# The last 64 tokens of a batch on both partition halves, from q@kv to x, and weights loaded by chunk halves

## The chip, the cores and the metric

The kernel runs on one core of a Trainium2 chip. The metric is the device time of one execution in microseconds (us). Before the change the median of 13 runs is 226.29 us, from 224.67 to 227.38.

## What is computed

Shapes: q, k, v are (8 batches, 8 heads, 576 tokens, 64). Linear attention without a softmax is normalized per head and token, the heads are joined to x (8, 576, 512), and x goes through an attention of four experts, of which each token takes the best two.

```python
kv = np.einsum('bhsd,bhse->bhde', k, v)
out = np.einsum('bhsd,bhde->bhse', q, kv)
rms = np.sqrt(np.mean(out * out, axis=-1, keepdims=True) + 1e-06)
x = (out / rms * g_norm).transpose(0, 2, 1, 3).reshape(B, S, H * D)

logits = x @ w_gate                      # (B, S, 4), the best two kept, softmax over them
for e in range(4):
    qe, ke, ve = x @ wq[e], x @ wk[e], x @ wv[e]          # 512 -> 64
    a = causal_softmax(qe @ ke.transpose(0, 2, 1) / 8)
    result += weight_of_expert_e * (a @ ve @ wo[e])
```

## The kernel before

The work is written as small tasks, each named by its kind, batch and part: `("out", b, i)` is q@kv of token block `i` of batch `b`. Three strings, found by a planner ahead of time, fix everything that a scheduler would decide: `ORDER` is the sequence in which all tasks are emitted (the order on each engine's queue follows from it), `ENGINE` gives one letter per task (V VectorE, A ScalarE, G GpSimd) for those that can run on more than one, and `SLOTS` the PSUM bank or buffer that each takes. `ZEROS` puts matmuls of zeros ahead of some tasks on TensorE. Tasks of several batches are interleaved.

The 576 tokens of a batch are four blocks of 128 and a last one of 64 (block index `NF` = 4, length `REM` = 64). The stages of a batch, with the names used by the profile:

- Loads: `lk`, `lv`, `lq` and the remainders `lkr`, `lvr` are DMAs issued by SyncE (SP), for batch 0 those of v by ScalarE. The weights are loaded once, during the first batches: `lw(nm, p)` loads the experts 2p and 2p+1 of wq, wk or wv into `w_stage`, and `ws` scales them by `g_norm` into `w_r`.
- `kv` (L405) sums k^T v over the tokens; `kvc`, `kgm`, `kgr`, `kgx` copy it into `kvx` with four gate columns per head (64 + 4 = 68 = `GW`). `kvx` holds each pair of heads (c, c+4) on the two partition halves with zeros in the other head's columns, so one matmul against 136 columns serves both heads.
- `q` (L448) and `qc` bring q to `qT`, with heads c and c+4 on the partition halves of chunk c. For batches from 2 on, `qc` alone does this by a VectorE transpose (L456).
- `out` (L466): per block four matmuls, one per chunk c, into two PSUM banks. The last block has 64 tokens, so its chunks 0, 1 go to partitions 0 to 63 and its chunks 2, 3 to 64 to 127. An fp32 matmul is two PE instructions in the profile.
- `oc` copies the block to `o_sb` (tokens on partitions; L283 is the ScalarE form of every such copy, L285 the VectorE form). For the last block these are two copies of 64x272, both into partitions 0 to 63. `sq` (L492, L496 on ScalarE, L498 on GpSimd) squares, `red` (L502) sums to `ms`.
- `ln`, `rs`, `na` to `nd` make 1/rms (`rstd`) of all blocks. `gl` and `lg` (L545, L551) make the gate's logits in `lg8`: gate columns times `rstd`, summed over the eight heads. Then `m8` (L584) finds the best two, and `sh`, `ex`, `md`, `mk`, `gt`, `den`, `rd`, `gate` make the weights that `iv` (L727) needs, after the scores of the batch.
- `xm` (L557, GpSimd) multiplies by `rstd` and permutes the features so that chunk c of x holds the features 4p + c; `x` (L567) transposes each chunk on TensorE by a matmul against the identity, and `xc` copies to `xT`.
- `v` (L626), `qp` and `kp` (L645) project x; `sc` (L672) are the scores, `exp` (L686) on ScalarE, `msk` (L692) on GpSimd, `pv` (L706), `rc`, `iv`, `oc2` (L723, L727, L734) scale, `ot` (L749) transposes, `y` (L764) projects out, `yc` copies, `st` stores.

For a block of 64 tokens `x` moves 64 columns in each of its four matmuls:

```python
p_t[:, c * P : c * P + nt], lhsT=tiles["x", b, i][:, c, :], rhs=ident_r[:, 0:nt], start=True, stop=True
```

and `proj` reads `xT` chunk by chunk against `w_r[nm][:, c, ...]`, so the order of features in x and in the weights' rows must agree.

Of the kernel before, what the change touches and what calls it, by code (L numbers as in the profile page):

```python
# [24 lines left out]
ZEROS = {("q", 0, 4): 8, ("gb",): 2, ("kv", 0, 2): 6, ("kv", 0, 1): 3, ("q", 0, 3): 3}  # L25

ORDER = (
    "090E010403080507020u060H0v003F0D0c0A0F0G3C0b0J0I0d0C0a0j0i0B0e0f0k390s0g3H0l0m0h0t381A0n163B1C1B1D0w3718170o19"
    "0y3A0x1Q0q1R0p0z1S1T3Y0U1U0r0+1V3Z3E1k1E1F1G12100-1H5f1h1I111l143U1m3G1J131Y151i3V3D1K1j1Z1L1M3L1a0S1N1O3K5g0V"
    "3I1P1W3S5l1b1X0K1n3J3T0Q1e3W3M3N0M3Q5i1q1o1r1p3X0T1c5e3O1f1s201g3P225c213q1d0L1+233r3R5d3e0R1-1t3a0N3f1u5b3g3i"  # L30
    "1v3b3h3m3c0W3s3d2W3j5j3t3n243k2X0O3o3l2UAS3p253u1y2V1w5h1z3v3w2e1x3x5r3y2f5m3z2b460X2Y2h885s2c4C5p2i2Z5k0P5q40"
    "4D5t5uAV474E4926485v8C43418D274A5w423+4S4B2d5n3-2E2g4T2H284F2F442a864I4U4G2I4J4H5y2G452B5o292k4V4K2j4L5x4Q2J2C"
    "2A2l802m4M2n4N4a2o4R2D2p2q2r2L0Y4b2KAR2P4Y2M2Q2N2R2O4y4Z854l4z4c4m814i4d4n4f5z4+5+4j844e5-4g4k4-89630Z4h836059"
    "6450615A535156826B6562575B6766525487586C6F68552SAa6D6G2s4O2T2t4W6H8A6E692x4X6A344P2yAZ316I4p35324o2z6J4t8H6K4u"
    "4q4v6L364r8G6M4s6N8N8F6O6d338E8MAX4w8I6X2+4x8B8J6e2-5D6U6f6Y308K2u6R6ZAW6V5H2v6t8L5I6a6W5J6S2w6u5CAT6T6P6r5E5F"
    "6Q6b6s6p6g6cCt6x5G6j6h6q6k6v6i6y8P6l7N6w6m8O7P7OCz6n8UAc6o7QAe8Y8VAU8W7a8Z7X7b7R7Y8Q7c8XAd7S7Z7U8R8g8a7TAY5K7V"
    "8b6-8hAb8S7W8c5L8i708TC-7d8d8j7e8e6z7fCs7i7j8f7gAi6+7hCxAh8k7k8l7A8m77Ao8n7BC+748o7C7871An8pAgCy8yAq72AfAp92Cv"
    "5Y758zAk8-7l5Z93Aj8+5V5a948v5PAl905QFU8q9I915W5R8s8wAm9J9K5X8x7m73Av8r769LCw7995AzAw9896D199977DAx9A8t9BCuA+7F"
    "Ay7GAr8uA-7H9C9QAs9DD0B0AtB59RFM7EAuB17ID3B67J9q7KHjB7DD9OB8B2HkD59rB3D69PD7HiB49bDC9YB99c9VBA9Z9d9SD2D4BB9T9a"
    "9ED8FHBC9oD99WBD9UBE9G9FBFFQDABT9M7L5M7M9HFJBN5S9p5NBU5T9N7wBQBGBV9-5UDB9s7xA09vBK9tBW9y7yDE7q9wBXBOBZDF5OBHBL"  # L40
    "BPBRHlBMBaA1DK9XBS9u9zBj9xDLHm9eBk9+9f7r9gDOFLBYDM9jA2BbDP7sA39k9hFODNBlDQBIFRA7A4BmBc9lDSA8DRA5BJFIBdA9BpBeDT"
    "A69iBnBqFKBhBoCFBiHnDGCGDWFTDHCDDXHqDIDJDYBfHuCEDUDZAA9mBg7nAB9nCQFPDVCNCRCK7oCSCOCHFXFNCICPFW7pFYCLCJFVFSDaCM"
    "ALDbFZDcCTDdFaAMHoCUDeACDfCYDlAFFbANAD7tAGBrDgAECVFcCWDhCZDiCaAHHyCXBsHxHr7uDoHzFeDuC07vDxBwC1FgBzBxHvBtDyFdD+"
    "HwDrB+FfDvHtD-AIH+ByBuFlB-DwAJHpDzC2FtE0H-BvAKC3FuE1FmC4HsFpI0FnFhFqE2FoE3FrFxI1C8C5C9FiC6FsAOFy7zFjAPDsCA7+AQ"
    "C7CbFzDpDtFkCBCc7-DmI3FvDqEAF+CCDjFwE8DkCgF-E9CpG0DnChCmI2CqCiG1EgCnG2I4CrG3G4I5CdG5EhCoEGEBG7CeG6CfGMCjGAEHI6"
    "CkGPGNIAClGQI7GOGJEEIBI8IMEFICECINI9ERGREDGDELIDESEOGSEMEIGTE6IOEJGKGUIEIPGGGLEPEeEKENIFEQE7IIEfIGETE4IHIJErE5"
    "ElIKEsEiEmEoEVEtILEjEUEnEZGEEaEWEbIQEXGBEpEkEYGHEcGFEqG8GIGCGZEdIRG9GbISGaITGXIUGcIVGdGYIWGVIbIXGfGeInIYGWH3Gg"
    "IqIoIrIpIkEvH4EuEzH5IsEwE+ItExE-IeEyIlH6IuF0IvIcImIhF1HGIdH7HHHAH8HIHDFEHEF5H9FFIyFGF6HBHFF8IzFBF9F7HCF2FCIiFA"
    "IZFDIjIfIaGhIgF3IwGiJ0F4IxGsJ1GpGtGjGqGuGmJWGkGrJ6GnJXGlJYGoJ7I+JZJ2I-J4J3GwJ5GvG+HKG-GxH0GyJHGzJaJIHJHOJbJJJj"
    "HPHLJgHQHMJkHNJcJhJBJlJEHRJCJiH1J8HSH2JFJDJdHfJ9JGHWHgHcHhJeJAHZHdJLHaJfHeJKHXJPJmJQHbJMJRJnJNJoHYJOJpJUHTJqJS"  # L50
    "JVJrJuJTJsHUJvJtHVJ-K2K0JwJyJxK1K3K8K4JzK5J+K6K7K9KA"
)
ENGINE = (
    "VAVAVAVAVAVVVVVVVVVVVGVVVVVGVGVVVAVAVVVVAVVVVVVVVAVAVAVAVAVVAVVVAVVAAVVVAVVAAVAAAGAGAAGGAGAAGGAGGVGVVGVVGVVGVV"
    "GVVVGAGGGVVGVVVVVVVVVVVVVVVAGVAGVAGVAGVVVGVVGVVVVAVVVAGVAGVAGVAGVVVGVVGVVAVAVVAVVAVVAVVVVVVVVVVVVVVVVVVVAVVAVV"
    "VAVAVVVVVAAVVAAVVAAVVAAVVAAVAAGGGGGVGVAGVAGVAGVAGVAVGAGGGVVGVAVAVVVVVAVAVVVAGVAGVAGVAGVVVGVVGVVAVVVVVAGVAGVAGV"
    "AGVVVGVVGVVVVAVVAVVAVVVVVAVVVVVVVVVVVVVVVVVVVAVVAVVVVVAGVVVGVVAAVVVGVVAGVAAGGGGGVGVAGVAGVAGVAGVAVGAGGGVVGVVVVV"
    "AVVVAVAVAVAGVAGVAGVAGVVVGVVGVVAVVVVVAGVAGVAGVAGVVVGVVGVVVVVVVAVVAVVVVVAVVVVVVVVVVVVVVVVVVVVVVVVVVVVVAVVAGVVVAV"
    "VAGVVVGVAAGGAGGVGVAGVAGVVGVAGVAVGAGGGVVGVVVVVVVVVVVVVVVAGVAGVAGVAGVVVGVVGVVAVVVVVAGVAGVAGVAGVVVGVVGVVVVAVVAVVV"
    "VVAVVVVVVVVVVVVVVVVVVVVVVAVVAVVVVVVGVVAAVVAGVVVAVVVAVAAAGGGGVGVAGVAGVAGVAGVAVGAGGGVVGVAVAVAVAVAVVVVVAGVAGVAGVA"  # L60
    "GVVVGVVGVVAVAVVVAGVAGVAGVAGVVVGVVGVVAVAVVAVVAVVAVVAVVVVVVVVVVVVVVVVVVVVVVAVVVVVAAVVVGVVVGVVAGVVVAVAAAGAGGVGVVG"
    "VVGVAGVAGVVVGAGGGVVGVVVAVAVVVAVVVVVAGVAGVAGVAGVVVGVVGVVVVVVAVAGVAGVAGVAGVVVGVVGVVVVVVVVVVVVVVVVVVVVVVVVVVVVVVV"
    "VVVVVVVVAVVVVVAGVVVGVVAAVVAGVVAGVAAAGAGGVGVVGVAGVAGVVGVAVGAGGGVVGVVVAVAVVVVVAVAVAGVAGVAGVAGVVVGVVGVVVVVVAVAGVA"
    "GVAGVAGVVVGVVGVVVVAVVAVVAVVVVVVVVVVVVVVVVVVVVVVVVVVVVVVVVVVVGVVAGVVAAVVAGVVAGVAAGGGGGVGVVGVVGVVGVVGVVVGAGGGVVG"
    "VAVVVVVAVVVAVAVAGVAGVAGVAGVVVGVVGVVVVVVVVAVAGVAGVAGVAGVVVGVVGVVVVAVAVVAVVVVVAVVVV"
)
# [9 lines left out]
def names(nb):  # L76
# [3 lines left out]
    for b in range(nb):  # L80
# [14 lines left out]
        out += [(m, b, g) for g in range(len(PARTS[b])) for m in ("ln", "rs", "na", "nb", "nc", "nd")] + [("gl", b), ("lg", b)]  # L95
# [23 lines left out]
def kernel(  # L119
# [61 lines left out]
    g_rows = const.tile([P, NCH], FP32, name="g_rows")  # L181
# [29 lines left out]

    kr, vr, kvx, lg8s, vexts, mss, sqs, rstds, roots = [], [], [], [], [], [], [], [], []
    for j in range(2):
# [14 lines left out]
        nc.vector.memset(t[REM:P, NF], 1.0)  # L228
# [9 lines left out]
    nc.gpsimd.memset(ob[REM:P, NF], 0.0)  # L238
# [17 lines left out]
    for j in range(2):  # L256
        t = const.tile([P, NB, 8], FP32, name=f"lg8_{j}")
        nc.gpsimd.memset(t[:], -1.0e30)
        lg8s.append(t)
        t = const.tile([P, NB, E, Hd + 1], BF16, name=f"vext{j}")  # L260
        nc.gpsimd.memset(t[:, :, :, Hd : Hd + 1], 1.0)
        nc.gpsimd.memset(t[REM:P, NF], 0.0)
        vexts.append(t)
# [12 lines left out]
    st = {}  # L276

# [70 lines left out]
    def gr():  # L348
        p_g = small("gr")
        nc.tensor.matmul(p_g[:, 0:Dh], lhsT=ones[0:1], rhs=g_row[:], start=True, stop=True)  # L350
        nc.tensor.matmul(
            p_g[:, Dh : Dh + NCH],
            lhsT=spread[:].rearrange("i a j -> i (a j)"), rhs=g_four[:], start=True, stop=True, skip_group_check=True,
        )
# [106 lines left out]
    def out_mm(b, i):  # L461
        p_o, nt = big("out", b, i), blocks[i][1]
        for c in (0, 2, 1, 3):

            p0 = 0 if nt == P else c // 2 * nt
            nc.tensor.matmul(  # L466
                p_o[p0 : p0 + nt, c // 2, c % 2 * 256 : c % 2 * 256 + 2 * GW],
                lhsT=qTs[b % NQT][:, c * S + i * P : c * S + i * P + nt],
                rhs=kvx[b % 2][:, c, :, :].rearrange("p a g -> p (a g)"),
                start=True,  # L470
                stop=True,
            )


    def p_out(b, i):
        nt = blocks[i][1]
# [396 lines left out]
```

## Time and profile before

| | |
|---|---|
| median of 13 runs | 226.29 us |
| lowest, highest | 224.67, 227.38 us |
| profiled execution | 227.14 us |
| its span (first to last instruction) | 225.4 us |
| granted TensorE clock | 0.995 |
| busy: TensorE, VectorE, ScalarE, GpSimd | 209.0, 157.7, 133.1, 125.7 us |
| DMA | 40.29 MB in 92576 packets |

PE is TensorE's matmuls, PEld its weight loads (which overlap them), DVE is VectorE, ACT ScalarE, POOL GpSimd, SP SyncE. A line number names the instruction in the kernel; a line such as L283 is a helper's and serves many tiles, so the tile (`o_sb<-p`) tells which. A row of a group gives, after the count, the busy time in us, the mean of one in ns, and the idle time ahead of them with what ended it. A row of the timeline gives start and length in us; instructions of one kind that follow each other are merged. Matmuls overlap, so what one costs in a run is the distance from start to start and not its own length.

### The profile page before, as it was taken

The page shows a single profiled execution, that of the slowest core. Times are in us where ns is not written, and L with a number is a line of the kernel's source. Part 1 is how long each engine was busy: PE and PEld are TensorE (multiplying, and loading weights), DVE is VectorE, ACT ScalarE, POOL GpSimd, SP SyncE. Part 2 cuts the span into 40 slices and gives each one's busy share as a digit, 9 for nine tenths or more (in the row PEclk, how much of TensorE's full clock was granted, in tenths as well). Part 3 has the DMA queues.
Part 4 walks back from the last instruction along what each step waited for, and adds up shares of the span by engine and source line. Part 5 has one row for each costly group of instructions (what it writes and reads, how often), then busy time and mean ns, then how long its engine had stood idle before and what let it go on. Part 6 is the DMA issues. An engine that isn't in the chain of part 4 may idle for free. (4 is left out here: it accounts for less than half of the span.)

```text
span 225.4 us, 6603 instructions
## 1 busy us (share of the span) xinstructions
PE 209.0 (93%) x2550; PEld 177.7 (79%) x2562; DVE 157.7 (70%) x366; ACT 133.1 (59%) x265; POOL 125.7 (56%) x278
## 2 busy tenths in 40 slices
PE   7788799998999789999999999999999999999991
PEld 2367697987998679897989699878868899799660
DVE  6175669748766779689796855689996476853671
ACT  0214742886579461858526864865764982655852
POOL 8400676069539662569715980469449959712530
PEclk9999999999999999999999999999999999999997
DMA  4988979998998986999999999798434000050056
GB/s 121 315 240 245 297 197 215 341 242 103 141 331 175 185 196 207 218 134 191 259 185 299 267 290 244 114 212 187 96 96 165 3 0 4 12 198 3 0 182 242
DMA packets 92576, 40.29 MB, mean 179 GB/s; under 512 B 66688, under 2 KB 88192, under 8 KB 92544
## 3 DMA queue, kind: packets, MB, share of 16 engines
q1 hardware_dynamic: 90704, 38.61, 72.1%
q10 hardware_dynamic: 1712, 1.25, 2.1%
q8 instruction: 20, 0.33, 0.7%
q14 instruction: 12, 0.10, 0.2%
q0 software_dynamic: 128, 0.01, 0.0%
HBM read 30.42 MB, written 9.44 MB: 177 GB/s over the span
## 5 line engine op out<-in xcount | busy, mean ns | idle before, releaser
L686 ACT ACTIVATE PT<-p 128x1024 bf16<-128x1024 f32 (+1 forms) x64 | 50.3, 842 | 7.0 <-PE p L672 6.6
L692 POOL TENSOR_SCALAR_AFFINE_SELECT PT<-PT 128x256 bf16<-128x256 bf16 (+1 forms) x80 | 29.1, 383 | 26.9 <-ACT PT L686 26.2
L557 POOL TENSOR_TENSOR x_tok<-o_sb,rstd 128x512 fp32r<-128x512 f32 x40 | 43.0, 1129 | 0.5
L466 PE MATMUL p<-kvx,qT 128*128 128x136 f32 (+1 forms) x320 | 39.2, 285 | 1.1 <-DVE kvx L285 0.7
L466 PEld LDWEIGHTS p<-kvx,qT 128*128 128x128 f32 (+1 forms) x320 | 34.7, 179 | 3.9 <-DVE kvx L285 0.9
L502 DVE TENSOR_REDUCE ms<-sq 128x8 f32<-128x520 f32 (+1 forms) x40 | 26.9, 684 | 7.1 <-POOL sq L498 3.6
L498 POOL TENSOR_TENSOR sq<-o_sb 128x512 f32<-128x512 f32 (+1 forms) x20 | 20.6, 1039 | 12.7 <-DVE ms L502 6.4
L626 PE MATMUL p<-wv_r,xT 128*128 128x256 f32 x160 | 25.1, 291 | 0.7 <-ACT xT L283 0.7
L567 PE MATMUL p<-ident_r,x_tok 128*128 128x128 f32 (+1 forms) x160 | 23.4, 279 | 1.0 <-DVE vext L285 0.3
L567 PEld LDWEIGHTS p<-ident_r,x_tok 128*128 128x128 f32 x160 | 20.6, 191 | 4.1 <-POOL x_tok L557 1.8
L283 ACT COPY o_sb<-p 128x544 f32<-128x544 f32 (+1 forms) x29 | 15.1, 532 | 13.0 <-PE p L466 12.6
L672 PE MATMUL p<-qTp,kT 64*128 64x64 f32 (+4 forms) x192 | 21.6, 341 | 1.1 <-DVE kT L285 0.4
L626 PEld LDWEIGHTS p<-wv_r,xT 128*128 128x128 f32 x160 | 20.8, 189 | 1.9 <-ACT xT L283 0.8
L405 PE MATMUL p<-v_b,k_b 128*64 128x64 f32 x512 | 20.7, 225 | 1.5 <-DMA k_b<-in_k_dram 1.5
L405 PEld LDWEIGHTS p<-v_b,k_b 128*64 128x64 f32 x512 | 18.2, 138 | 4.1 <-issue 2.4
L645 PE MATMUL p<-xT,wk_r 128*128 128x288 f32 x128 | 20.9, 306 | 0.1
L764 PE MATMUL p<-wo_b,OT 128*128 128x512 bf16 (+1 forms) x85 | 18.2, 343 | 1.7 <-issue 0.5
L645 PE MATMUL p<-xT,wq_r 128*128 128x288 f32 x128 | 19.8, 300 | 0.0
L645 PEld LDWEIGHTS p<-xT,wk_r 128*128 128x128 f32 x128 | 17.6, 188 | 1.7 <-DVE xT L285 0.5
L672 PEld LDWEIGHTS p<-qTp,kT 64*128 64x128 f32 x192 | 14.2, 185 | 5.9 <-ACT PT L686 1.1
L456 DVE STREAM_TRANSPOSE qT<-q_b 128x576 f32<-128x576 f32 x24 | 17.5, 755 | 2.0 <-DMA q_b<-in_q_dram 2.0
L285 DVE COPY o_sb<-p 128x544 f32<-128x544 f32 (+1 forms) x19 | 12.0, 629 | 9.5 <-PE p L466 4.2
(113 smaller groups left out, 346.4 us busy)
## 6 DMA issues: line engine op xcount, KB each, us to landing
k_b<-in_k_dram SPq DMA_DIRECT2D x14, 512.0 KB, 6.5
v_b<-in_v_dram SPq DMA_DIRECT2D x14, 512.0 KB, 6.4
out_dram<-y SPq DMA_DIRECT2D x28, 256.0 KB, 2.8
q_b<-in_q_dram SPq DMA_DIRECT2D x48, 144.0 KB, 5.0
q_b<-in_q_dram SPq DMA_DIRECT2D x16, 128.0 KB, 4.1
k_b<-in_k_dram SPq DMA_DIRECT2D x4, 256.0 KB, 5.3
v_b<-in_v_dram ACTq DMA_DIRECT2D x4, 256.0 KB, 5.3
k_rem<-in_k_dram SPq DMA_DIRECT2D x16, 64.0 KB, 5.0
```

The source lines that it names most:

```text
L405: nc.tensor.matmul(p_kv[hh * Dh : (hh + 1) * Dh, c, :], lhsT=lhs, rhs=rhs, start=(j == 0), stop=(j == NF), skip_group_check=True,)
L466: nc.tensor.matmul(p_o[p0 : p0 + nt, c // 2, c % 2 * 256 : c % 2 * 256 + 2 * GW], lhsT=qTs[b % NQT][:, c * S + i * P : c * S + i * P + nt] ...
L498: nc.gpsimd.tensor_tensor(out=dst, in0=src, in1=src, op=AluOpType.mult)
L502: nc.vector.tensor_reduce(mss[b % 2][:nt, i, :], sqs[(NB * b + i) % 3][:nt], axis=AX_X, op=AluOpType.add)
L557: nc.gpsimd.tensor_tensor(out=buf(("x", b, i), [P, NCH, P], FP32R, "x_tok")[:].rearrange("p c (h r) -> p h r c", h=H), in0=ob[:, i, :, 0:D ...
L567: nc.tensor.matmul(p_t[:, c * P : c * P + nt], lhsT=tiles["x", b, i][:, c, :], rhs=ident_r[:, 0:nt], start=True, stop=True)
L626: nc.tensor.matmul(p_v[:, 0 : E * Hd], lhsT=blocks_of(xTs[b % 2], c)[:, i * P : (i + 1) * P], rhs=w_r["v"][:, c, :, :].rearrange("p e f -> ...
L645: nc.tensor.matmul(p_p[:, s, 0:HALF], lhsT=w_r[nm][:, c, 2 * pr : 2 * pr + 2, :].rearrange("p e f -> p (e f)"), rhs=blocks_of(xTs[b % 2], ...
L672: nc.tensor.matmul(p_s[:, el, o : o + hi - lo], lhsT=kTs[(2 * b + pr) % 3][pp, kb * P : (kb + 1) * P], rhs=tiles["qTp", b, pr][pp, lo:hi], ...
L686: nc.scalar.activation(PT[:, :, d0 : d0 + o], big("sc", b, pr, j)[:, :, 0:o], ACTF.Exp, scale=scale)
L692: nc.gpsimd.affine_select(out=d, in_=d, compare_op=AluOpType.is_ge, fill=0.0, base=0, pattern=[[0, 2], [1, w]], channel_multiplier=-1,)
L764: nc.tensor.matmul(p_y[o * nq : (o + 1) * nq, 0:w], lhsT=lhs, rhs=wo_b[:, pr, o * w : (o + 1) * w], start=(pr == 0), stop=(pr == EP - 1), ...
```

## The change

From q@kv to x, the last block of a batch now has its heads 0 to 3 on partitions 0 to 63 and its heads 4 to 7 on partitions 64 to 127.

- `out` of that block: for each chunk two matmuls of 68 columns, one per head of the pair, to the two partition halves of one PSUM bank (eight instead of four).
- `oc`: one copy of 128x272 instead of two of 64x272. `sq` and `red` work on four heads of 128 partitions. The columns of heads 4 to 7 of that block are set once: 0 in `o_sb`, 1 in `ms`.
- The gate's logits of that block are then two partial sums on two partition halves. Two new tasks join them: `ls` copies the upper half down (ScalarE), `la` adds it (GpSimd), between `lg` and `m8`.
- The features are ordered by halves: chunk 2a + s holds the features 256a + 2p + s. So `xm` is one instruction per four heads: two for a full block, one for the last. `x` of the last block is two matmuls of 128 columns, one per s, and `xc` takes the halves apart.
- The weights follow: `lw(nm, a)` loads feature half a of all four experts, 512 bytes in a row instead of 1024; `g_rows` has two columns instead of four.
- `ORDER`, `ENGINE`, `SLOTS` and `ZEROS` are new throughout. `ZEROS` has 39 matmuls instead of 22, 22 of them ahead of `gb`.

```diff
-ZEROS = {("q", 0, 4): 8, ("gb",): 2, ("kv", 0, 2): 6, ("kv", 0, 1): 3, ("q", 0, 3): 3}
+ZEROS = {
+    ("gb",): 22, ("kv", 0, 1): 10, ("kv", 0, 2): 3, ("out", 0, 4): 3, ("kv", 1, 3): 1,
+}
...
-    def lw(nm, p):
+    def lw(nm, a):
         nc.sync.dma_start(
-            buf(("x", nm, p), [P, 2, NCH * Hd], FP32, "w_stage")[:],
-            w_dram[nm][2 * p : 2 * p + 2].rearrange("e (p c) f -> p e (c f)", c=NCH),
+            buf(("x", nm, a), [P, E, 2 * Hd], FP32, "w_stage")[:],
+            w_dram[nm][:, a * D // 2 : (a + 1) * D // 2, :].rearrange("e (p s) f -> p e (s f)", s=2),
         )
...
     def out_mm(b, i):
...
+        nt = blocks[i][1]
+        for c in range(NCH):
+            lhs = qTs[b % NQT][:, c * S + i * P : c * S + i * P + nt]
+            if i < NF:
+                nc.tensor.matmul(
+                    big("out", b, i)[:, c // 2, c % 2 * 256 : c % 2 * 256 + 2 * GW], lhsT=lhs,
+                    rhs=kvx[b % 2][:, c, :, :].rearrange("p a g -> p (a g)"), start=True, stop=True,
+                )
+                continue
+
+            for a in range(2):
+                nc.tensor.matmul(
+                    small("out", b, i)[a * nt : (a + 1) * nt, c * GW : (c + 1) * GW], lhsT=lhs, rhs=kvx[b % 2][:, c, a, :],
+                    start=True, stop=True, skip_group_check=True,
+                )
...
+    def heads(i):
+        return H if i < NF else NCH
...
     def red(b, i):
-        nt = blocks[i][1]
-        nc.vector.tensor_reduce(mss[b % 2][:nt, i, :], sqs[(NB * b + i) % 3][:nt], axis=AX_X, op=AluOpType.add)
+        n, sq = heads(i), sqs[(NB * b + i) % 3]
+        nc.vector.tensor_reduce(mss[b % 2][:, i, 0:n], sq[:, 0:n], axis=AX_X, op=AluOpType.add)
...
+    def lg_shift(b):
+        nc.scalar.copy(lg_other[b % 2][:], lg8s[b % 2][REM:P, NF, 0:E])
+
+    def lg_add(b):
+        t = lg8s[b % 2][0:REM, NF, 0:E]
+        nc.gpsimd.tensor_tensor(out=t, in0=t, in1=lg_other[b % 2][:], op=AluOpType.add)
+
     def xm(b, i):
-        nc.gpsimd.tensor_tensor(
-            out=buf(("x", b, i), [P, NCH, P], FP32R, "x_tok")[:].rearrange("p c (h r) -> p h r c", h=H),
-            in0=ob[:, i, :, 0:Dh].rearrange("p h (r c) -> p h r c", c=NCH),
...
+        t = buf(("x", b, i), [P, NCH, P], FP32R, "x_tok")
+        for a in range(heads(i) // NCH):
+            hs = slice(a * NCH, (a + 1) * NCH)
+            nc.gpsimd.tensor_tensor(
+                out=t[:, 2 * a : 2 * a + 2, :].rearrange("p s (l r) -> p l r s", l=NCH),
+                in0=ob[:, i, hs, 0:Dh].rearrange("p l (r s) -> p l r s", s=2),
...
     def x_tr(b, i):
-        p_t, nt = small("x", b, i), blocks[i][1]
-        for c in range(NCH):
+        for c in range(heads(i) // 2):
             nc.tensor.matmul(
-                p_t[:, c * P : c * P + nt], lhsT=tiles["x", b, i][:, c, :], rhs=ident_r[:, 0:nt], start=True, stop=True
+                small("x", b, i)[:, c * P : (c + 1) * P], lhsT=tiles["x", b, i][:, c, :], rhs=ident_r[:], start=True, stop=True
             )
```

## The prediction, made before the changed kernel was run

> **What bounds the kernel now.** I read the page first, then the windows by stage, the chain of waits, the groups by shape, and last the timeline where single shapes stand alone. The page:
>
> ```profile
> span 225.4 us, 6603 instructions
> ...
> PE 209.0 (93%) x2550; PEld 177.7 (79%) x2562; DVE 157.7 (70%) x366; ACT 133.1 (59%) x265; POOL 125.7 (56%) x278
> ```
>
> TensorE (PE) is busy 93% of the span, VectorE (DVE) 70%, ScalarE (ACT) 59%, GpSimd (POOL) 56%. The windows say where the other 7% lies:
>
> ```profile
> 0.00:20.00 20.00, 15.62 (x171) 9.45 (x173) 10.36 (x39) 4.38 (x9) 7.17 (x25) 1.00 0.81 228
> ...
> 155.00:165.00 10.00, 9.45 (x108) 8.36 (x110) 9.88 (x22) 7.32 (x14) 6.92 (x15) 1.00 0.47 89
> 165.00:215.00 50.00, 49.23 (x489) 41.91 (x491) 31.55 (x77) 32.74 (x61) 31.15 (x70) 1.00 0.15 52
> ```
>
> The columns after the length are PE, PEld (weight loads), DVE, ACT, POOL, clock, DMA share and GB/s. PE idles in the first 20 us, which wait for data; from 165 to 215 it is busy 49.2 of 50 us. Between 155 and 165 another engine sets the pace: DVE is busy 9.88 of 10 us. The chain of waits shows the same from the other side, PE groups throughout except in one such stretch:
>
> ```profile
> 158.97 1.02 PE p L466 x8
> ...
> 161.59 0.10 issue
> 161.68 0.38 ACT o_sb L283
> ...
> 162.48 0.37 ACT y L283
> 162.85 0.24 ACT xT L283
> ```
>
> So a PE instruction saved after the first 20 us is worth nearly its own pace, and a copy saved on DVE or ACT is worth something only in stretches like 155 to 165.
>
> **The change, part by part.** (1) *x_tr of the last block*, TensorE. Before: four matmuls of 64 columns per batch; after: two of 128. What counts is the pace, start to start:
>
> ```profile
> 26.44 0.53 PEld L567 LDWEIGHTS p<-ident_r,x_tok 128*128 128x128 f32 x4
> ...
> 28.23 0.97 PEld L567 LDWEIGHTS p<-ident_r,x_tok 128*128 128x128 f32 x8 [0.37 <-issue]
> ```
>
> One load lasts 0.19 us. Four take 0.53, so (0.53-0.19)/3 = 0.113 us each; eight (0.97-0.19)/7 = 0.111. The four are the 64-column shape, the eight the 128-column shape: the pace doesn't depend on the columns. Two fewer per batch are 8 x 2 x 0.112 = 1.8 us. Batch 0's fall into the stretch that waits for data, so I count seven batches: -1.6 us. A rule speaks against this: the Trainium skill, "TensorE: Matmul & The Clock Gate", section "Back-to-back issue gap", gives an isolated gap of about 60 cycles up to 64 columns and 134 for 128. By it four narrow and two wide cost nearly the same, and this term would be 0. The rows above show no difference between the widths, so I keep -1.6; the rule's end is the rival "no saving".
>
> (2) *out_mm of the last block*, TensorE. Before, eight instructions of 136 columns (an fp32 matmul is two), in pairs on two column halves of the array; after, sixteen of 68.
>
> ```profile
> 173.86 0.68 PE L466 MATMUL p<-kvx,qT 128*64 128x136 f32 x8
> 174.47 0.74 PE L626 MATMUL p<-wv_r,xT 128*128 128x256 f32 x4
> ```
>
> The eight take 0.61 us to the next group. The nearest row to the new shape is on the chain, L405, pairs of 64 columns on the same halves:
>
> ```profile
> 144.79 2.48 PE p L405 x80
> ```
>
> That is 2.48/80 = 31 ns each, so sixteen are 0.50, and with 68 columns 0.53. The eight, without the 0.15 us at the switch back to the full array, are 0.46. Ends: 0 (the columns are the same in sum) and +0.07 us per batch; I take +0.1 us in all, +0.5 at the far end.
>
> (3) *Evacuation and norm of the last block*, DVE and ACT.
>
> ```profile
> L502 DVE TENSOR_REDUCE ms<-sq 64x8 f32<-64x520 f32 x8 | 5.4, 673 | 2.8 <-ACT sq L492 1.6 <-POOL sq L498 0.9 <-ACT sq L496 0.2
> ...
> L283 ACT COPY o_sb<-p 64x272 f32<-64x272 f32 x10 | 3.8, 380 | 2.0 <-PE p L466 1.9
> ...
> L285 DVE COPY o_sb<-p 64x272 f32<-64x272 f32 x6 | 2.6, 431 | 0.8 <-PE p L466 0.8
> ```
>
> Sixteen half copies become eight (ten to five on ACT, six to three on DVE, by the new engine string): ACT -1.9 us, DVE -1.3. The reduce goes from 520 to 260 elements; between 0.673 us at 520 and the 0.161 us of the 20-element reduce of L611 that is 0.41, so DVE -2.1. The square (0.63 us on ACT, 1.03 on POOL) drops to about 0.38 and 0.6.
>
> (4) *Reassignments.* Counting the letters of both engine strings and giving each task its row, the new plan moves much from DVE to ACT (thirty instead of 24 of the xT copies, eleven instead of six of the kT copies, 26 instead of 20 squares on ACT) and two weight scalings from POOL to DVE. With (3): DVE 158 to about 145 us, ACT 133 to about 145. In the stretches where DVE sets the pace this should help; PE's waits on DVE add up to 4.2 us on the waits view, 2.8 of them before 25 us. Of the remaining 1.4 I take a fifth: -0.3 us. Ends: -3 (155 to 165 runs at PE's pace) and +4.6 (the rival on ACT).
>
> (5) *xm*, POOL. Each full block becomes two instructions of 256 elements instead of one of 512, the last block one of 256.
>
> ```profile
> 77.13 4.14 POOL L557 TENSOR_TENSOR x_tok<-o_sb,rstd 128x512 fp32r<-128x512 f32 x4
> ...
> 86.25 0.23 POOL L596 TENSOR_TENSOR g_mk<-lg,g_m 128x20 f32<-128x20 f32 x1 [1.46 <-DVE g_m L584]
> 86.44 0.23 POOL L587 TENSOR_TENSOR g_sh<-lg,g_m 128x20 f32<-128x20 f32 x1
> ```
>
> 512 elements have a pace of about 1.01 us ((4.14-1.1)/3), 20 elements 0.19 (86.25 to 86.44): 1.67 ns per element and 0.16 us fixed. Two halves are 2 x 0.585 = 1.17. So +0.16 us x 32, -0.43 x 8: POOL +1.7 us. Here a rule is milder than the rows: the Trainium skill, "GPSIMD Engine Reference", section 2.1 "Instruction dispatch", puts the dispatch at tens of cycles per instruction. By that the split would cost a third or less of the 0.16 us. Neither enters the sum: what hides it is that only three waits of x_tr on x_tok, 1.8 us in all, are seen on PEld; without cover the five blocks of a batch come 0.2 us later, 1.7 us over eight batches.
>
> (6) *Gate chain.* After the reduce into lg8, an ACT copy of 64x4 (ls, nearest row L283 64x16: 0.203 us) and a POOL add of 64x4 (la, nearest row L727 128x4: 0.203) come ahead of max8. Behind ls in ACT's queue stand exps and copies, behind la on POOL the masks and xm; each can be held until DVE's reduce, and then ACT's copy, is done. The gate itself is needed by iv alone: in the trace it is ready 8.6 us (batch 2) to 31 us (batch 6) before its first use, so the 0.4 us and two handovers are covered: 0. Uncovered they would be about 0.6 us in one batch.
>
> (7) *Weights by chunk halves.* Six DMAs as before, 512 B per packet instead of 1024. The trace's packets average 56 ns at 1024 B and 29 at 512 B: 1536 x 56 = 86 against 3072 x 29 = 89 us, over 16 engines +0.2 us, not awaited. 0.
>
> (8) *The order at the start.* SP's and ACT's loads are permuted. K and V of batch 1 are complete after 6.1 MB issued before, after 6.9 MB now. In the trace the last piece lands at 28.4 us; 0.77 MB more at the 249 to 288 GB/s of the windows 20 to 30 is about 2.9 us. PE starts kv of batch 1 at 29.3. The new order puts two more transposes of q (0.95 us each) and one x_tr less (0.45) ahead of it, so it would arrive at 30.7 and the data at 31.3: +0.5 us. Ends: -1 (the other waits of the first 25 us, 5.5 us of idle PE, shrink) and +2.9. The added zero matmuls (39 instead of 22) fill waits and count 0.
>
> Sum: -1.6 +0.1 -0.3 +0.5 = -1.3 us. The profiled execution took 227.14 us, 1.74 around its span of 225.4; it would become 225.8. The median of the 13 runs lies 0.85 lower, at 226.29: 225.0 us, -0.6%. A change under 0.5% (1.13 us) can hardly be told from none in this kernel, whose runs spread from 224.67 to 227.38.
>
> **The rivals.** *ACT becomes the pacer* (slower). ACT gets 12 us more, and it already holds 16.0 of 20 us between 40 and 60. In the chain's stretch from 160.0 to 163.9 its queue leads; PE then starts some 21 small matmuls worth 1.6 us, so the stretch costs 2.3 us. Two more like it, and the sum is +3.3: 229.6 us; one only gives 227.3. It decides where ACT is busy over nine tenths of 10 us while x or out stands in PE's order. For it: 30 of 40 xT copies now go through ACT. Against: DVE's relief is as large, and ACT averages 64%.
>
> *DVE's relief is worth more* (faster): 155 to 165 and the waits at 16 to 24 us vanish, -2.3 on top: 222.7 us. For it speaks 9.88 of 10 us; against, that DVE is under 8 tenths in most windows.
>
> *No saving, or the start takes it*: the pace of x_tr isn't kept when two stand alone, or data of batch 1 come 2.9 us late: 226.3 us, and up to 227.7.
>
> **How the numbers follow.** Forecast case 0.45 (its own range 223.6 to 226.2), DVE's relief 0.12, no saving 0.15, ACT 0.28. Under 225.16 lie DVE's case and 0.33 of the forecast case: faster 0.45. Between 225.16 and 227.42: 0.12 of the forecast case, 0.08 of "no saving": same 0.20. ACT's case and 0.07 of "no saving" make slower 0.35. The range 222.6 to 229.4 leaves out the outer halves of the end cases.
>
> **What would show it.** Right: L567 with 144 instructions instead of 160 at 0.11 us pace; last-block L466 sixteen to a batch within 0.55 us before the next group; DVE and ACT both near 145 us; PE busy about 207 us plus what the longer run of zero matmuls adds at the start; no wait of iv on the gate. Wrong: PE idle above 20 us, with ACT lines (L283) as releasers in the waits of PE and PEld; a chain that lies on ACT for more than 10 us before 210; kv of batch 1 later than 32 us; x_tr waiting on POOL for more than 4 us.

## The result, and the profile after

The changed kernel is slower. In the first job it took 230.57 us (median of 11 runs) beside 226.55 us for the kernel before, a ratio of 1.0138 with a 95% interval of [1.0101, 1.0174]; in a second job (r1 below) 227.85 us, ratio 1.0078 [1.0045, 1.0111]. Forecast were 225.0 us. Times are medians over all executions of a job, ratios compare undisturbed executions alone, and since the execution profiled in the first job (231.65 us) was a disturbed one, the profile read here is that of r1, the same kernel: 227.15 us, span 225.4. Its page:

```profile
span 225.4 us, 6752 instructions
...
PE 211.8 (94%) x2614; PEld 180.0 (80%) x2627; DVE 147.9 (66%) x347; ACT 144.2 (64%) x293; POOL 118.7 (53%) x308
```

DVE is down from 157.7 to 147.9 us and ACT up from 133.1 to 144.2, as counted (both "near 145"). The windows that carried the prediction, in the same columns:

```profile
0.00:20.00 20.00, 17.00 (x183) 10.31 (x183) 9.10 (x33) 3.86 (x8) 6.92 (x25) 1.00 0.78 222
155.00:165.00 10.00, 9.95 (x177) 8.59 (x177) 9.21 (x20) 7.33 (x17) 4.16 (x11) 1.00 0.62 203
165.00:215.00 50.00, 49.08 (x502) 41.91 (x505) 26.41 (x67) 37.62 (x72) 30.10 (x78) 1.00 0.15 51
```

From 155 to 165 us PE is now busy 9.95 of 10 us, where it was 9.45. But other work stands there now: the kv of batch 7 begins at 161.3 us in r1 and at 151.1 us in the kernel before, and VectorE is still busy 9.21 of the 10 us. So this window can't show that the stretch in which VectorE led is gone. The groups that the change touches (instruction, count, busy us, mean ns, idle ahead and its releaser):

```profile
L587 PE MATMUL p<-ident_r,x_tok 128*128 128x128 f32 x144 | 21.6, 286 | 0.3 <-ACT PT L711 0.3
...
L578 POOL TENSOR_TENSOR x_tok<-o_sb,rstd 128x256 fp32r<-128x256 f32 x72 | 43.0, 658 | 0.2
...
L479 PE MATMUL p<-kvx,qT 128*64 128x68 f32 x128 | 5.8, 229 | 0.1
...
L609 DVE MAX8 g_m<-lg 128x8 f32<-128x8 f32 x40 | 3.8, 154 | 3.1 <-POOL lg L572 3.0
...
L572 POOL TENSOR_TENSOR lg<-lg,lg_other 64x4 f32<-64x4 f32 x8 | 1.7, 212 | 5.5 <-ACT lg_other L568 5.5
L568 ACT COPY lg_other<-lg 64x4 f32<-64x4 f32 x8 | 1.5, 192 | 2.3 <-DVE lg L561 2.3
```

x_tr is L587 now, 144 instructions instead of 160. The last two rows are the new gate steps: 0.2 us each, as priced, but over the eight batches GpSimd stood 5.5 us in front of its add and VectorE 3.0 us in front of max8.

So the parts have about the size that was counted, and the kernel is slower. PE's busy time didn't fall, it rose from 209.0 to 211.8 us: the zero matmuls take 9.7 us instead of 6.1, and without them it is 202.2 instead of 202.9. The prediction had about 207 us plus those zeros. The experiments ask two things: why a shorter PE program gives nothing, and what the rest costs.

### The profile page after: what moved, and what is told of

It reads as the page before. It is cut to its first block, busy times and chain, and to the rows that moved or that the text cites. A ratio compares the mean times of both kernels' runs of the same rounds, so it can differ in the third digit from the quotient of the medians.

```text
span 229.9 us, 6752 instructions
## 1 busy us (share of the span) xinstructions
PE 213.2 (93%) x2614; PEld 180.6 (79%) x2627; DVE 147.6 (64%) x347; ACT 144.4 (63%) x293; POOL 118.7 (52%) x308
## 4 chain that ended last, share of the span: by engine, by line
PE 53%; DMA 11%; DVE 11%; ACT 9%; SPq 9%; issue 3%; POOL 2%; ACTq 0%; DVEq 0%; POOLq 0%
PE p L670 11%; PE p L472 9%; PE p L651 6%; PE p L411 5%; PE p L789 5%; PE p L697 5%; PE p L731 4%; PE p L587 4%; DMA wo_st<-in_moe_wo_dram 4%; ACT PT L711 3%; SPq L328 3%; SPq L312 3%; PE p L454 2%; DMA k_b<-in_k_dram 2%; ACT xT L289 2%
## 5 line engine op out<-in xcount | busy, mean ns | idle before, releaser
L578 POOL TENSOR_TENSOR x_tok<-o_sb,rstd 128x256 fp32r<-128x256 f32 x72 | 43.1, 656 | 0.2
L717 POOL TENSOR_SCALAR_AFFINE_SELECT PT<-PT 128x256 bf16<-128x256 bf16 (+1 forms) x80 | 29.3, 382 | 25.6 <-ACT PT L711 23.0
L472 PE MATMUL p<-kvx,qT 128*128 128x136 f32 x256 | 34.4, 285 | 0.1
L472 PEld LDWEIGHTS p<-kvx,qT 128*128 128x128 f32 x256 | 31.3, 190 | 1.1 <-DVE kvx L291 0.3
L512 DVE TENSOR_REDUCE ms<-sq 128x8 f32<-128x520 f32 (+1 forms) x40 | 24.7, 633 | 7.5 <-ACT sq L506 5.6
L587 PE MATMUL p<-ident_r,x_tok 128*128 128x128 f32 x144 | 21.3, 284 | 0.4 <-POOL lg L572 0.4
L587 PEld LDWEIGHTS p<-ident_r,x_tok 128*128 128x128 f32 x144 | 18.4, 191 | 3.2 <-issue 0.6
L508 POOL TENSOR_TENSOR sq<-o_sb 128x512 f32<-128x512 f32 (+1 forms) x14 | 14.4, 1035 | 10.5 <-DVE o_sb L291 5.2
L289 ACT CAST xT<-p 128x512 fp32r<-128x512 f32 (+1 forms) x30 | 16.0, 562 | 5.7 <-PE p L587 4.2
L670 PEld LDWEIGHTS p<-xT,wk_r 128*128 128x128 f32 x128 | 17.7, 188 | 1.4 <-DVE o_sb L291 0.7
L731 PE MATMUL p<-vext,PT 128*128 128x65 bf16 x480 | 17.8, 193 | 0.8 <-ACT xT L289 0.8
L789 PE MATMUL p<-wo_b,OT 128*128 128x512 bf16 (+1 forms) x84 | 17.4, 344 | 0.8 <-issue 0.2
```

Source lines behind the costliest of these rows:

```text
L472: nc.tensor.matmul(big("out", b, i)[:, c // 2, c % 2 * 256 : c % 2 * 256 + 2 * GW], lhsT=lhs, rhs=kvx[b % 2][:, c, :, :].rearrange("p a g ...
L512: nc.vector.tensor_reduce(mss[b % 2][:, i, 0:n], sq[:, 0:n], axis=AX_X, op=AluOpType.add)
L578: nc.gpsimd.tensor_tensor(out=t[:, 2 * a : 2 * a + 2, :].rearrange("p s (l r) -> p l r s", l=NCH), in0=ob[:, i, hs, 0:Dh].rearrange("p l ( ...
L587: nc.tensor.matmul(small("x", b, i)[:, c * P : (c + 1) * P], lhsT=tiles["x", b, i][:, c, :], rhs=ident_r[:], start=True, stop=True)
L670: nc.tensor.matmul(p_p[:, s, 0:HALF], lhsT=w_r[nm][:, c, 2 * pr : 2 * pr + 2, :].rearrange("p e f -> p (e f)"), rhs=blocks_of(xTs[b % 2], ...
L717: nc.gpsimd.affine_select(out=d, in_=d, compare_op=AluOpType.is_ge, fill=0.0, base=0, pattern=[[0, 2], [1, w]], channel_multiplier=-1,)
```

## The experiments

Ratios below are to the kernel before, run in the same job, with 95% intervals. The theory of the prediction: PE paces, so PE time counts nearly in full, and the loss is the new plan's (its start, or ACT as the pacer). Its rival: the edit itself costs, because what it adds holds up queues in which other work stands, and PE time is worth little. Each expectation says in its own words what it weighs.

**Edit and plan crossed.** r1 is the changed kernel again. r2 is the edit under the old plan, r3 the old data path under the new plan.

```diff
 # r2: the edit, with ORDER, ENGINE, SLOTS, ZEROS of before
+        if n[0] == "lg": out += [("ls", n[1]), ("la", n[1])]
 # (weights still loaded by expert pairs, in 512-byte packets)
 # r3: the data path of before, with ORDER, ENGINE, SLOTS, ZEROS of after
+    return [n for n in order if n[0] not in ("ls", "la")], engine
 # (out of the last block in one PSUM bank)
```

> The changed kernel once more, beside the others on one chip. Every theory: 229.5 us, 1.3% over the kernel before (its runs so far: 1.0138).

> The edit of the data path (last block on both partition halves, xm in halves, ls and la, 512 B packets of weights) with the old plan: order, engines, slots and zero matmuls of the kernel before, ls and la put directly behind lg; the weights stay split by pairs of experts. Theory 'new plan': the edit alone is the forecast's gain, -1.3 to -1.9 us, so 224.9 us (0.993), and PE's lost time stays that of before. Theory 'edit': the halves of xm and the longer gate chain cost more than x_tr saves, so 228 to 230 us (1.01 to 1.015), with POOL waiting on the copy of the logits.

> The data path of before (four narrow x_tr matmuls, two half copies, one xm, no ls and la) with the new plan: order, engines, slots and zero matmuls of the changed kernel. Theory 'new plan': the plan alone costs about 5 us, and without the edit's gain this is slower than the changed kernel: 231 to 232 us (1.02). Theory 'edit': 226 to 227 us (1.00).

Measured: r1 227.85 us, 1.0078 [1.0045, 1.0111]. r2 229.05 us, 1.0100 [1.0056, 1.0144]. r3 232.14 us, 1.0271 [1.0230, 1.0313]. The edit by itself is slower by 1.0%, with the plan that the kernel before was tuned with. The new plan by itself, with the path it wasn't made for, is slower by 2.7%. r2 came out as the theory 'edit' had it, r3 as the theory 'new plan' had it. Both together cost 0.8 to 1.4%, less than the sum and less than the plan alone, so the two don't add up, and the crossing doesn't say which of them the changed kernel pays for.

**Single parts of the edit, put into the kernel before.** r4: only the two gate steps (adding zeros). r5: only xm of a full block in two halves. r6: only the PE saving, two of the last block's four x_tr left out (chunks 2 and 3, so the features 4p + 2 and 4p + 3 of the last 64 tokens are missing from x) and the other two 128 columns wide. r11: the reverse, the last block's x_tr done twice.

```diff
 # r4, at the end of lg(b)
+        nc.scalar.copy(lg_other[b % 2][:], lg8s[b % 2][REM:P, NF, 0:E])
+        nc.gpsimd.tensor_tensor(out=t, in0=t, in1=lg_other[b % 2][:], op=AluOpType.add)
 # r5, xm
+        for hs in (slice(0, NCH), slice(NCH, H)) if i < NF else (slice(0, H),):
 # r6, x_tr
-        for c in range(NCH):
+        for c in range(NCH if i < NF else 2):
 # r11, x_tr
+        for _ in range(1 if i < NF else 2):
             for c in range(NCH):
```

> The kernel before with one part of the edit: the ScalarE copy (ls) and the GpSimd add (la) behind lg, here adding zeros. Theory 'cover' (the prediction's step 6): 226.3 us, 1.00. Theory 'queue': the two wait for each other in ACT's and POOL's queues and hold up exps, masks and xm behind them: 228 to 229 us (1.01), most of the 1.010 that the edit cost under the old plan.

> The kernel before with another part alone: xm of the four full blocks as two GpSimd instructions of 256 elements (the last block stays one of 512). POOL gets 0.16 us x 32 = 5 us more. Theory 'cover' (step 5): under 0.3%. Theory 'POOL paces x': 0.65 us later per batch at the x stage, up to 5 us, 1.01 to 1.02.

> The kernel before with two of the four x_tr matmuls of the last block left out (the other two 128 columns wide, so xT's last 64 tokens come from two chunks only). This is the saving of step 1 alone under the old plan. Theory 'PE paces': -1.6 to -1.8 us, 0.992 to 0.993. Theory 'PE waits instead': the freed time goes into the next wait, 0.998 to 1.000.

> The kernel before with the last block's four x_tr matmuls done twice: 4 x 0.112 us more on TensorE per batch, 3.6 us in all. Theory 'PE paces': 1.014 to 1.016. Theory 'PE's own time is not what sets the end' (two fewer gave nothing): under 1.005.

Measured: r4 227.96 us, 1.0088 [1.0054, 1.0122]: two steps of 0.2 us per batch cost nearly all of the edit's 1.0%. r5 228.09 us, 1.0027 [0.9973, 1.0080]: no cost that can be told from none, up to 0.8% at the end of the interval. r6 226.91 us, 1.0007 [0.9965, 1.0048]: no gain. r11 227.59 us, 1.0074 [1.0045, 1.0104]: 3.6 us more of PE work cost 1.7 us, between the ranges of its two theories. The prediction's first step falls with r6, and its premise is halved by r11.

**Do the transfers pace?** A third theory came up here, called A in these expectations: in the kernel before the DMA share is 0.91 to 1.08 in every window from 20 to 140 us, so loads and stores might pace the first 160 us and hide PE's savings. r12 to r14 cut the bytes of the stores (half or more of the rows of batches 0 to 3 aren't written) and repeat r6 and r11 on top; r15 cuts them in the changed kernel, r18 in the edit under the old plan.

```diff
 # store(b, qc), in r12 to r15 and r18
+            n = 32 if b < 4 else nq
-            eng.dma_start(out[b, s0 : s0 + nq, ...], y_t(b, qc)[o * nq : (o + 1) * nq, 0:w])
+            eng.dma_start(out[b, s0 : s0 + n, ...], y_t(b, qc)[o * nq : o * nq + n, 0:w])
```

> The kernel before, with the stores of batches 0 to 3 writing only 32 of each block's 64 or 128 rows (same instructions, same waits, 2.65 MB less before the last load and 3.5 MB less in all; those rows of the output are not written). Theory A, the loads and stores pace the first 160 us: about 34.5 MB move by then, so 7.7% fewer bytes bring the last load forward by up to 12 us, as far as PE's own work allows; 215 to 222 us, ratio 0.95 to 0.98. Theory B, PE's queue paces and the transfers only keep up with it: 226 to 227 us, ratio 0.997 to 1.003.

> The kernel of r12 with two of the four x_tr of each last block left out (the other two 128 columns wide), which is the PE saving of the change by itself: 16 x 0.112 = 1.8 us. Under the full stores it was worth nothing (1.0007). Theory A: with the transfers relieved PE paces, and this run is 1.2 to 1.8 us below r12. Theory B, the saving falls into PE idle time whatever the transfers do: equal to r12 within 0.6 us.

> The kernel of r12 with each last block's four x_tr done twice: +32 x 0.112 = 3.6 us of PE work, which cost 1.7 us under the full stores. Theory A: 3 to 3.6 us above r12. Theory B: about 1.7 us above r12, as before.

> The changed kernel with the same cut in its stores. If what it loses is that its plan moves the loads on more slowly (30.2 MB by 140 us where the kernel before had 31.6), the loss goes with the cut: equal to r12 or up to 1.5 us below it, since its PE work is 1.6 us less. If the loss sits in its gate chain and queue orders, it stays: 1.7 to 3 us above r12.

> The edit under the old plan (r2, 1.010) with the stores of batches 0 to 3 cut to 32 rows as in r12 (1.000). If the edit's cost under the old plan is its gate chain on ScalarE and GpSimd, it has nothing to do with transfers and stays: 1.008 to 1.011. If it is lost to late transfers as the changed kernel's seems to be (1.0078 to 1.0025 with the cut), it falls to 1.002 to 1.005.

Measured: r12 226.20 us, 0.9998 [0.9964, 1.0032]. A falls: 36.89 MB instead of 40.29 MB change nothing. r13 226.74 us, 0.9985 [0.9940, 1.0031], against r12 a ratio of 0.9987: the saving doesn't appear when the transfers are relieved either. r14 227.24 us, 1.0065 [1.0030, 1.0100], the same half price as r11. r15 226.78 us, 1.0025 [0.9991, 1.0059]; r18 228.30 us, 1.0124 [1.0069, 1.0179]. So the edit's loss under the old plan stays when the bytes of the stores are cut (r18). Of the changed kernel's loss a part seems to go with them: r15 is 0.6 us above r12, where its two theories had 0 or less and 1.7 to 3 us. That rests on comparing two jobs, and the intervals of r1 and r15 still overlap a little.

**The start, the gate steps and the last load in the new plan.** r7 moves the loads of the remainders of batch 1 back; r8 leaves ls and la out (the logits of the last 64 tokens come from heads 0 to 3 alone); r9 and, under the old plan, r10 have both on VectorE; r16 loads the second half of K of batch 7 earlier; r17 is r9 and r16 together.

```diff
 # r7: order, behind ("lq", 0, 2)
+    order[at:at] = [("lkr", 1), ("lvr", 1)]
 # r8
+    return [n for n in order if n[0] not in ("ls", "la")], engine
 # r9, r10
-        nc.scalar.copy(lg_other[b % 2][:], lg8s[b % 2][REM:P, NF, 0:E])
+        nc.vector.tensor_copy(out=lg_other[b % 2][:], in_=lg8s[b % 2][REM:P, NF, 0:E])
-        nc.gpsimd.tensor_tensor(out=t, in0=t, in1=lg_other[b % 2][:], op=AluOpType.add)
+        nc.vector.tensor_tensor(out=t, in0=t, in1=lg_other[b % 2][:], op=AluOpType.add)
 # r16, r17
+    order.remove(("lk", 7, 1))
+    order.insert(order.index(("lk", 7, 0)) + 1, ("lk", 7, 1))
```

> The changed kernel with its remainder loads of batch 1 (lkr, lvr: four DMAs of 64 KB, not needed before kv of batch 1) moved behind the load of q's block 2 of batch 0. Theory 'start': the new order's loads make out of batch 0 begin at 21 us instead of 18; with these out of the way it begins about 1 us earlier and the kernel is 1 us faster than the changed one (1.004 to 1.008 over before instead of 1.008 to 1.014). Theory 'later stages': no change against the changed kernel.

> The changed kernel (new plan) without ls and la: the last 64 tokens' gate logits come from heads 0 to 3 alone, everything else stays. Theory 'gate chain' (its two ops cost 0.9% in the old plan and as much here): 0.998 to 1.003 over before. Theory 'the rest of the edit or the start': 1.008 or more, as the changed kernel.

> The changed kernel with ls and la on VectorE, the engine of the reduce before and of max8 after them, so that no queue waits for another. Theory 'queue' (what costs is the handover DVE, ACT, POOL, DVE with other work behind it in each queue): most of the cost is gone, 1.001 to 1.005. Theory 'length' (the gate comes later): as the changed kernel, 1.008 to 1.012.

> The edit under the old plan (run r2, 1.010) with ls and la on VectorE. Theory 'queue': 1.000 to 1.003, the best form of the edit, and perhaps as fast as before. Theory 'length': 1.008 to 1.012.

> The changed kernel with the second half of K of batch 7 loaded right behind the first half, ahead of ten loads and stores that SP issues before it now. In the changed kernel this load lands last, at 160 to 163 us, and the kv of batch 7 starts at 161 to 166 us where the kernel before starts it at 151. Theory A, the changed kernel's loss is this order of its last transfers: the ratio goes from 1.008 to 1.002 or below (226.3 to 227.0 us). Theory B, the loss sits in its queues and gate chain, and a late load only takes the place of other waits: 1.006 to 1.009 as r1.

> Both mends of the changed kernel at once: K of batch 7 earlier as in r16, and the two instructions that bring the logits of heads 4-7 across the partitions on VectorE instead of ScalarE and GpSimd (1.0053 alone). Theory A: the two add up, 1.000 or below (225.5 to 226.5 us). Theory B: 1.004 to 1.007, as with the chain's move alone.

Measured: r7 228.09 us, 1.0071 [1.0034, 1.0108]. r8 227.86 us, 1.0073 [1.0040, 1.0105]. r9 227.97 us, 1.0053 [1.0017, 1.0088]. r10 228.31 us, 1.0072 [1.0037, 1.0107]. r16 228.57 us, 1.0135 [1.0088, 1.0183]. r17 230.44 us, 1.0153 [1.0090, 1.0216]. None of these mends the changed kernel, and several went past what was expected. r16 and r17 lie above the ranges of both their theories (1.009 and 1.007 at most): the late load of K of batch 7 is not the loss. r7 lies in its theory's range and in the interval of r1, so its time decides nothing. r9 is just past the range of 'queue' (1.005), with an interval that overlaps r1's; r10 misses 'queue' (1.003 at most), and is lower than r2 with overlapping intervals. So moving both steps to VectorE doesn't bring the time back. r8 misses its theory 'gate chain' (1.003 at most) and is the one that surprises: under the new plan the gate steps can be left out and the time stays.

The kernel before remains the fastest of all that compute the reference.

## Where a saving on PE goes

The kernel before, r6, r11, r13 and r14 emit the same tasks in the same order. So every task of PE can be found in both traces and its starts subtracted. The table follows each last block's x_tr: how much later (+) or earlier (-) than in the kernel before PE begins its next task, and what is left 7 to 10 us on (both against the shift just ahead of x_tr; us). The row of r12, which leaves x_tr as it is, is the control.

```
x_tr at (us)       26.5   50.3   79.8  103.7  125.4  154.8  177.1  192.2    sum
r13 right behind  -0.20  -0.18  -0.19  -0.20  -0.19  -0.19  -0.19  -0.01
r12 left           0.00  +0.76   0.00  -0.32  +0.02  -0.01   0.00  +0.02
r6  left           0.00  -0.03  +0.01  -0.32  +0.03   0.00  -0.23  +0.02   -0.5
r13 left          +0.01  -0.03   0.00  -0.32  +0.02  -0.02  -0.22  -0.01   -0.6
r11 left          +0.25  -0.12  +0.35   0.00  +0.29  -0.01  +0.45  +0.29   +1.5
r14 left          +0.25  -0.09  +0.33  -0.01  +0.30   0.00  +0.43  +0.28   +1.5
```

In seven batches PE does leave x_tr 0.2 us earlier. A few us later the lead is gone in six of them. The -0.32 at 103.7 is not the saving's, for r12 has it without any saving: the profiled execution of the kernel before waits there for an `x_tok`, and r6, r11, r12, r13 and r14 don't. Its row:

```profile
105.43 0.63 PE L567 MATMUL p<-ident_r,x_tok 128*128 128x128 f32 x4 [0.28 <-POOL x_tok L557]
```

In the same way the +0.76 of r12 at 50.3 is a wait of that execution alone, for a weight. With -0.32 as the zero of its column, what is left sums to -0.2 us for r6 and -0.3 us for r13, where the prediction had -1.6, and to +1.8 us for r11 and r14, which cost 1.7 and 1.5 us by the clock. Single runs of this kernel spread by 2 us and more, while r6 and r13, and r11 and r14, agree to 0.03 us. But all rows are taken against one execution of the kernel before, and what happened to that one stands in every row: only the control tells it apart.

Where the lead ends can be read in the timeline of batch 0 (start, length, engine, line, out<-in, shape, count, idle time with its releaser). First the kernel before, then r6, which stands 0.05 us later here:

```profile
26.46 0.62 PE L567 MATMUL p<-ident_r,x_tok 128*128 128x64 f32 x4
27.01 1.09 PE L448 MATMUL p<-ident_f,q_b 128*64 128x128 f32 x16
27.70 0.41 DVE L285 CAST xT<-p 128x256 fp32r<-128x256 f32 x1
28.26 0.52 PE L567 MATMUL p<-ident_r,x_tok 128*128 128x128 f32 x3 [0.16 <-DVE xT L285]
```

```profile
26.51 0.42 PE L567 MATMUL p<-ident_r,x_tok 128*128 128x128 f32 x2
26.86 1.09 PE L448 MATMUL p<-ident_f,q_b 128*64 128x128 f32 x16
27.75 0.42 DVE L285 CAST xT<-p 128x256 fp32r<-128x256 f32 x1
28.31 0.52 PE L567 MATMUL p<-ident_r,x_tok 128*128 128x128 f32 x3 [0.35 <-DVE xT L285]
```

The transposes of q (L448) start 0.20 us sooner against x_tr, the next x_tr not at all: it waits for VectorE's copy of xT, which stands behind a copy and a reduce that haven't moved. PE's wait grows from 0.16 to 0.35 us. A PE that is busy 93% of the time can still be led by others at every few us; the waits are short and spread, so no line of the waits view shows them as a sum.

## Where the edit's cost comes from

The same subtraction for the edit under the old plan, r2 and r18, shows three steps behind 100 us, the same in both: +0.47 and +0.46 us at 111 us, +0.61 and +0.63 at 128, +0.47 and +0.48 at 153; and one gain, -0.25 and -0.26, where x_tr of batch 6 is shorter. Together that is +1.3 us in both. Against r12, which doesn't have the wait at 105.4 us, the first step is +0.76 in both and the sum +1.6. By the clock r2 lost 2.3 us; what it lost ahead of 100 us I didn't follow. Each of the three steps can be followed in the trace.

*At 111 us.* The waits of the gate's exponential on ScalarE, in the kernel before and in r2 (us in total, times, longest):

```profile
ACT g_ex L593 <- POOL g_sh L587: 1.0, 3, 0.4
```

```profile
ACT g_ex L624 <- POOL g_sh L618: 4.1, 6, 0.8
ACT lg_other L574 <- DVE lg L567: 4.0, 5, 1.9
POOL lg L578 <- ACT lg_other L574: 3.7, 5, 1.7
```

And the timeline of r2 there:

```profile
106.70 0.19 POOL L578 TENSOR_TENSOR lg<-lg,lg_other 64x4 f32<-64x4 f32 x1 [0.73 <-ACT lg_other L574]
106.84 1.12 POOL L723 TENSOR_SCALAR_AFFINE_SELECT PT<-PT 128x256 bf16<-128x256 bf16 x3
...
108.12 0.22 POOL L618 TENSOR_TENSOR g_sh<-lg,g_m 128x20 f32<-128x20 f32 x1
...
108.37 0.22 ACT L624 ACTIVATE g_ex<-g_sh 128x20 f32<-128x20 f32 x1 [0.83 <-POOL g_sh L618]
...
108.50 0.61 ACT L512 ACTIVATE sq<-o_sb 128x512 f32<-128x512 f32 x1
...
109.02 0.59 ACT L293 COPY o_sb<-p 128x544 f32<-128x544 f32 x1
...
109.51 0.59 ACT L293 CAST xT<-p 128x512 fp32r<-128x512 f32 x1
...
110.15 0.53 PE L676 MATMUL p<-xT,wk_r 128*128 128x288 f32 x2 [0.49 <-ACT xT L293]
```

The add waits 0.73 us on GpSimd, with three masks behind it in the queue; `g_sh`, behind the masks, starts 2.39 us after the reduce into lg (105.73), in the kernel before 1.38 (107.34 to 108.72). The exponential stands in ScalarE's queue ahead of a square and two copies and waits 0.83 us for `g_sh`, where it had no wait in the kernel before; the copy of xT behind it comes late, and PE waits for xT.

*At 128 us* (seen at 125.5 in r2) the copy of xT stands right behind the new copy in ScalarE's queue, which waited 0.24 us for VectorE's reduce and took 0.2 us itself; PE waits 0.33 us for that xT. *At 153 us* it is GpSimd's queue:

```profile
150.46 0.19 POOL L578 TENSOR_TENSOR lg<-lg,lg_other 64x4 f32<-64x4 f32 x1 [0.30 <-ACT lg_other L574]
...
150.61 0.20 POOL L758 TENSOR_TENSOR inv<-inv,gate 128x4 f32<-128x4 f32 x1
...
150.84 0.89 DVE L765 TENSOR_TENSOR osc<-p,inv 128x256 bf16<-128x256 f32 x2 [0.72 <-POOL inv L758]
...
151.65 0.75 DVE L295 CAST kT<-p 128x576 fp32r<-128x576 f32 x1
...
152.45 0.69 PE L703 MATMUL p<-qTp,kT 64*128 64x64 f32 x6 [0.43 <-DVE kT L295]
```

The add stands ahead of the second `inv` of another batch; `osc` on VectorE waits 0.72 us for it (0.23 in the kernel before); behind `osc` stands the copy of kT, and PE's scores wait 0.43 us for that. None of the three goes through the gate's weights, whose lateness the prediction had weighed.

With both steps on VectorE (r10) 0.7% of the loss remains, and its trace has steps too: against r12 +0.3 us at 111, +0.4 at 128, +0.45 at 153, and +0.5 at 172 where r2 had 0.1. At 153 us it is VectorE's own queue now: the copy (0.18 us, at 151.53) and the add (0.52 us, at 151.75) stand ahead of `osc` (152.20) and of the copy of kT (153.00), and PE waits 0.40 us for that kT. Moving the steps moved the queue that they hold up.

**In the changed kernel** the new plan gives these steps other places, and r8 shows that taking them out then frees nothing that intervals of 0.3% to each side can show: the same kinds of waits stand there without them. These are rows of the waits view of r1, then of r8:

```profile
DVE lg L561 <- POOL gl L555: 7.2, 3, 5.3
...
ACT g_ex L618 <- POOL g_sh L612: 5.4, 3, 3.4
```

```profile
POOL g_mk L621 <- DVE g_m L609: 9.1, 2, 5.4
ACT g_ex L618 <- POOL g_sh L612: 6.4, 3, 3.1
DVE lg L561 <- POOL gl L555: 6.8, 2, 5.1
```

In one batch VectorE waits 5.3 us for gl from GpSimd with the gate steps, and 5.1 us without. That this lateness of the gate is what the changed kernel pays for is not shown: no run takes it away. Nor can it be read from two profiles alone, since the profiled executions of r1 and of the kernel before last the same 227.1 us. r15's time says that a part seems to go with the bytes of the stores, but its trace doesn't say where: in r1's profile PE's matmuls wait for a load only once, 0.83 us for q at 17.7 us, and r15's profile runs a steady 0.65 us ahead of r1's from 47 us to the end. The one place that was traced is in r7. Its kv of batch 5 starts at 115.7 instead of 116.9 us, the 1.2 us won at the start, but then PE waits for a remainder of V:

```profile
116.83 0.51 PE L415 MATMUL p<-v_rem,k_rem 128*64 128x64 f32 x3 [0.41 <-DMA v_rem<-in_v_dram]
```

Right behind this kv 0.4 us of the lead are left, by 131 us nothing, and the first k projection of that batch starts at 136.0 us in both. How the changed kernel's 0.8 to 1.4% divides between loads, the order of its queues and the rest of the edit stays open.

## Why the prediction was wrong, step by step

Two steps failed. Step (1) took a saved PE instruction for worth nearly its own pace, and it was worth nearly nothing. Step (6) took the two gate steps for covered, and under the old plan they cost 2.0 us. The two make up most of what the edit under the old plan missed its forecast by. For the changed kernel itself they do not suffice: r8 is as slow without the gate steps, and the cause of its own 0.8 to 1.4% stays open in part.

- *(1) x_tr, -1.6 us.* The pace was right (0.112 us an instruction, 16 fewer), the step from pace to time was not. r6 measured +0.1 ± 0.4%, the shifts give -0.2 us. The failing sentence is "a PE instruction saved after the first 20 us is worth nearly its own pace": it took a 93% busy PE for one that nobody leads. The Trainium skill has its rule on the issue gap ("TensorE: Matmul & The Clock Gate", "Back-to-back issue gap") for an isolated matmul, and says in the same section that in a stream of weight loads and matmuls both set the spacing; the rows here are of that second case, and show the same pace for 64 and 128 columns. The term of 0 that the prediction worked out from the rule came near the measured worth, but for another reason: the saving is there, and is lost in the next wait.
- *(2) out, +0.1 us.* Right: the chain gives 0.62 us from the sixteen to the next group, the eight took 0.61. The sign "within 0.55 us" had left out the switch back to the full array.
- *(3), (4) Fewer and reassigned copies, -0.3 us.* The loads of DVE and ACT came out as counted. No gain is seen, and none can be read from 155 to 165 us, where other work stands now. The rival "ACT becomes the pacer" had a price, 229.6 us, that lies near the first job's 230.57, but what it said would happen is not seen: ACT is busy 64%, and PE's waits for ACT add up to 2.4 us, 2.3 before.
- *(5) xm in halves, 0.* Consistent with r5 (1.0027, interval across 1). The rows of xm are busy 43.0 us before and after, where +1.7 was forecast. From start to start two halves take 1.14 us, one whole 1.01: 0.13 us more for the split, near the 0.16 that the rows gave and not a third of it.
- *(6) Gate steps, 0.* Wrong, and the largest miss under the old plan: r4 puts them at +0.88%, 2.0 us. Looked at were the gate's result and its slack of 8.6 to 31 us. The step named what stands behind ls and la, and then priced only the chain itself. The intermediate steps have no slack: the exponential waits already in the kernel before (1.0 us in three batches). "Uncovered 0.6 us in one batch" was the right size for one place; there are three such places behind 100 us alone, and they add.
- *(7) 512-byte packets, 0.* Not separated by a run of its own; r2 has them, and r4 accounts for nearly all of r2.
- *(8) The start, +0.5 us.* kv of batch 1 begins at 32.3 us in r1, 31.3 was forecast, 29.3 was before; by the prediction's own sign, "later than 32 us", this was wrong. r7 gives 1.2 us of it back until batch 5, and the end doesn't move. The start's time is not added to the end's, so the step was off by its size and in its use.
- *The new plan as a whole* was given +0.2 us, by (4) and (8). With the old path it costs 2.7% (r3), and no run shows which part of the plan does that.
- *The rival "no saving"*, with 226.3 to 227.7 us, was the nearest to r1's 227.85; it lacked the gate steps. No rival had a queue held up by a small step as its mechanism.

## What to carry to other kernels

A busy share of 93% doesn't make an engine the pacer: follow one saving for some us in the timeline and see what the engine waits for next; if a copy on another engine stands there that the saving doesn't move, the saving is lost in that wait. Price a small added step by what stands behind it in each in-order queue that it enters, and by the intermediate steps that it delays, not by the slack of its final result. Two kernels with one order of tasks can be compared task by task: differences of 0.03 us repeat where the medians spread by 2 us. But one accident of the execution that all are compared with looks like a repeated result, so put a second trace without the change beside them.

## What the runs showed of the hardware that was not expected

Between kernels of one plan, PE's starts follow each other alike to a few hundredths of a us over tens of us; the difference between executions comes in jumps, nearly all at a kv, where PE meets its loads (between the profiles of the kernel before and of r6 1.4 us at 78 us and 0.6 us at 119 us, where the kernel before waits 1.5 us in all for K). And 3.4 MB of stores less moved nothing (r12), though the DMA share of the kernel before stands near 1.0 for 120 us: a DMA share of 1.0 was no sign here that bytes pace.
